# A state-space block followed by a feed-forward block: where three GpSimd steps and three groups of transfers stand in a hand-written order

## The chip, the cores and the metric

The kernel runs on one core of one Trainium2 chip. The metric is the device time of one launch in microseconds; the time before is the median of three runs.

## The reference

Two blocks, one after the other. The first is a chunked state-space scan over 4 sequences with 8 heads each, 768 positions, head width 32, state width 16. The second is a feed-forward layer over the 3072 tokens that come out of it (256 wide, 2048 hidden). Cut to what matters:

```python
for c in range(nc):                      # chunks of positions, state carried along
    L = np.exp(cum[..., :, None] - cum[..., None, :]) * causal
    M = np.einsum('bhin,bhjn->bhij', Cc, Bc) * L
    y_intra = np.einsum('bhij,bhjd->bhid', M, xc)
    y_inter = np.einsum('bhin,bhnd->bhid', Cc, state) * decay_to_i
    y[:, :, sl] = y_intra + y_inter
    state = decay_full * state + sum_over_j(Bc * decay_from_j, xc)
...
x = y.transpose(0, 2, 1, 3).reshape(B * S, H * D)
h = x @ w_in
out = (h * np.cos(h)) @ w_out
```

## The kernel before, in words

**Tiling.** Positions are cut into 6 chunks of 128, and each chunk into two units of 64, so that there are units 0 to 11. A unit holds 64 positions of all 4 sequences, which is 256 tokens. The feed-forward layer is cut into 96 steps `n`, 16 to a chunk: step `n` takes the 256 tokens of one unit and 256 of the 2048 hidden columns. Chunk 1 (units 2 and 3) is the chunk of steps 16 to 31.

**One step of the feed-forward layer.** `first(n)` (L663) multiplies by w_in on TensorE into `hp`. `wind` (L670 on ScalarE, L676 on VectorE) and `gate` (L685, ScalarE) make the cosine, and `gated` (L690, VectorE) multiplies to `gT`. Two steps later, `second(n)` multiplies by w_out. From step 16 on it is `seven` (L771): the product of two-by-two blocks is made with seven instead of eight multiplications. For these, four combinations of the blocks of w_out, `wd[0]` to `wd[3]` (they live in buffers called `words` in the profile), are made once on GpSimd by `differ_w` (L709), each in two halves, `fore` (columns j 0 to 3) and `hind` (j 4 to 7); and three instructions of `differ` on GpSimd (L715, L717, L718) make the combinations `gd` of `gT` for each step. Inside `seven` the products come in the order 1, 2, 6, 7, 5, 4, 3: the first two need no combination, 6 needs the result of L717, 4 needs `wd[3]`, 3 needs the result of L718. `seven(20)` is the first that reads the `hind` halves; it runs in step 22.

**The scan's part around the change.** Of each unit `k`, two VectorE scans (`decays0`, L375) make its decays `lam`, and `weigh0(k)` (L381, GpSimd) makes `sc`, which is B weighed by the decay to the unit's end. `sums(k)` (L477, TensorE) multiplies `sc` with x to the unit's share of the state. `finish0(3)`, in step 22, runs the products with the old state (L516), then `sums(3)`, `sums(4)` and `sums(5)`, then the products inside the unit (L530). `add`, called in step 23, makes the state after unit 3 on GpSimd (L558, L565); half of it has to go to other partitions, which the four transfers at L567 do (the "exchange"). The result is read by `add_state(4)` (L499, VectorE) in step 28 and `open2(2)` (L621, then `sums(6)` and `sums(7)`, TensorE) at the end of step 29.

**What sets the order.** The order of every engine's instructions is written out by hand, in the loop over `n` at the end of the function; nothing is rescheduled. Nearly all transfers are issued by the sync engine (SP), in that same written order, and a transfer that has to wait for something holds up those behind it. `differ_at` says in which step each half of `differ_w` comes (after `gated(n)` and what follows it). `first_decays` puts the decays of units 4 and 5 in steps 17 to 20, and `decays2` calls `weigh0` as soon as a unit's second scan is written. `load(c, i)` loads B and x of chunk `c` in four parts; for chunk 3 they come in steps 22, 24, 25 and 26, for later chunks in the first four steps of a chunk. The names that the change touches are `load`, `add` inside `finish0`, `differ_at`, `decays2`, and two places in the loop.

Of the kernel before, what the change touches and what calls it, by code (L numbers as in the profile page):

```python
# [25 lines left out]
def kernel(  # L26
# [12 lines left out]
    nc = tc.nc  # L39
# [87 lines left out]
    def load(c, i):  # L127
        if c < NC:
            for s in range(2):
                (load_x if i // 2 else load_b)(2 * c + i % 2, s)  # L130

    def group(q, s):
        return slice(32 * (q ^ s), 32 * (q ^ s) + 32)
# [245 lines left out]
    def weigh0(k):  # L379
        scs[k] = sc = scan.tile([P, 2 * H, N], FP32, tag="sc0", bufs=3, name="sc0")  # L380
        G.tensor_tensor(out=sc, in0=bs[k].rearrange("p q (h n) -> p (q h) n", h=H),  # L381
                        in1=lams[k].rearrange("p q h i -> p (q h) i")[:, :, W - 1:W]
                        .to_broadcast([P, 2 * H, N]), op=ALU.mult)
# [119 lines left out]
    def finish0(k):  # L503

        m, xk = m_of[k], xrs[k]
        y = [pair("y") for _ in range(2)] if k else [pair("y")]
        at_ = [[(y[t][:, s, p * W:(p + 1) * W] if k else
                 y[0][:, s, t * P + p * W:t * P + (p + 1) * W]) for p in range(2)]
               for t in range(2) for s in range(2)]
        if k:  # L510
            old = states0.pop(k)
            for p in range(2):
                for s in range(2):
                    for q in range(4):
                        r, c0 = slice(32 * q, 32 * q + 32), W * (q % 2)
                        PE.matmul(at_[2 * (q // 2) + s][p][c0:c0 + W], lhsT=old[r, s, p],  # L516
                                  rhs=rTs[k][r, 2 * p + s], start=(p == 0), stop=False,
                                  tile_position=(32 * q, c0), skip_group_check=True)
        sums(k, [y[0][:, s, 3 * P:] for s in range(2)], lambda q, s: slice(32 * q, 32 * q + 32),
             start=(k == 0))  # L520
        if k == 3:
            at = [y[1][:, s, 2 * P:] for s in range(2)]
            for i in range(2):
                sums(4 + i, [ap[:, i * P:(i + 1) * P] for ap in at], group)
        for p in range(2):
            for t in range(2):
                for s in range(2):
                    ss = slice(s * W, (s + 1) * W)
                    for q in range(4):
                        PE.matmul(at_[2 * t + s][p][32 * q:32 * q + 32],  # L530
                                  lhsT=xk[ss, p, 4 * t + q], rhs=m[ss, p, 4 * t + q],
                                  start=False, stop=True,
                                  tile_position=(s * W, 32 * q), skip_group_check=True)
        if k % 2 == 0:
            yT[k // 2] = two.tile([P, 2, 2, 2 * P], FP32, tag="yT", name="yT")
        t_ = yT[k // 2][:, k % 2]
        if k:
            for t in range(2):
                ACT.copy(out=t_[:, t].rearrange("p (s i) -> p s i", s=2), in_=y[t][:, :, 0:P])
        else:  # L540
            ACT.copy(out=t_.rearrange("p t (s i) -> p s t i", s=2),
                     in_=y[0][:, :, 0:2 * P].rearrange("p s (t i) -> p s t i", t=2))
        if k == 3:
            take_sums(2, at)
        states0[k + 1] = new = states.tile([P, 2, 2, 2 * D], FP32, tag="state0", bufs=2,
                                           name="state0")

        def take():
            for t in range(2):
                ts = slice(t * D, (t + 1) * D)  # L550
                ACT.activation(new[:, :, :, ts], y[0][:, :, 3 * P:].rearrange(
                    "p s (q d) -> p s q d", q=2)[:, :, :, ts], AF.Copy, scale=slot[:, t:t + 1])

        def add():
            dec = scan.tile([P, 2, 2, 2 * D], FP32, tag="whole", bufs=1, name="whole")
            r4 = reachs[k].rearrange("p (q s) i -> p s q i", s=2)
            for s in range(2):
                G.tensor_tensor(out=dec[:, s], in0=old[:, s],  # L558
                                in1=r4[:, s, :, W:].to_broadcast([P, 2, 2 * D]), op=ALU.mult)
            if k < 3:  # L560
                G.tensor_tensor(out=new, in0=new, in1=dec, op=ALU.add)
                return
            whole = states.tile([P, 2, 2, 2 * D], FP32, tag="state1", bufs=1, name="state1")
            for s, to_ in ((1, new), (0, whole)):
                G.tensor_tensor(out=to_[:, s], in0=new[:, s], in1=dec[:, s], op=ALU.add)  # L565
            for q in range(4):
                nc.sync.dma_start(out=whole[group(q, 1), 1], in_=new[group(q, 0), 1])  # L567
            after[3] = whole
        return take, add

    def reaches(c, b):
# [302 lines left out]
    def store_a(dst, src):  # L874
# [4 lines left out]
    piece = {n: ("in", (n + 3) // 2) if n % 2 else ("out", n // 2) for n in range(NF)}  # L879
    fore, hind = slice(0, NJ // 2), slice(NJ // 2, NJ)  # L880
    differ_at = {NF - 2: [(0, fore), (1, fore)], NF - 1: [(2, fore), (3, fore)],
                 **{NF + i + i // 3 * 2: [(i, hind)] for i in range(4)}}

# [3 lines left out]
    def units_at(n, i):  # L889
        return [k for k, at in unit_at.items() if at[i] == n]  # L890
# [45 lines left out]
    def decays2(k, p):  # L936
        decays0(k, p)
        if p == 1:
            if k + 2 < 2 * NC:
                load_arow(k + 2)  # L940
            if k != 2 * NC - 1:
                weigh0(k)

    def reaches2(c, s):
# [61 lines left out]
    for n in range(AHEAD, NC * NF + LAG):  # L1006
        c, f = divmod(n, NF)
        if n < NC * NF:

            if c > 0 and f in (loads_of := (6, 8, 9, 10) if c == 1 else (0, 1, 2, 3)):  # L1010
                load(c + 2, loads_of.index(f))
            if n in (NF - 4, NF - 3):
                load_arow(n - NF + 8)
            if n == NF - 2:
                for k in (4, 5):
                    for s in range(2):
                        load_x(k, s)
            if n in (NF - 1, NF):
                load_along(2, (2 * (n == NF), 2 * (n == NF) + 1))
            for e, i in chunks_at(n, "along"):  # L1020
                load_along(e + 1, (2 * i, 2 * i + 1))
            first(n)
            closing = f == NF - 1 and 1 <= c < NC - 1
            take_y = finish2(c + 1) if closing else None
            wind(n)
            if closing:
                take_y(0)
            for e, s in chunks_at(n - 1, "turn"):
                turn2(e, s)
            for k in units_at(n, 2):  # L1030
                turn_unit(k)
            if n + 1 in piece:
                rests_of.append(grade(*piece[n + 1], later=True))
            gate(n)
            while len(rests_of) > (n == AHEAD):
                rest = rests_of.pop(0)
                if rest:
                    rest()
            joins = n in piece and piece[n] in held
            if joins:  # L1040
                join(*piece[n])

            behind = [lambda at=at: decays2(*at) for at in decays_at(n)]
            behind += [lambda c=c, i=i: add_state(2 * c + i) for c, i in chunks_at(n, "state")
                       if 2 * c + i < 2 * NC - 1]
            behind += [lambda at=at: reaches2(*at) for at in chunks_at(n, "reach")]
            behind += [lambda at=at: turn_blocks(*at) for at in chunks_at(n, "turn")]
            behind += [lambda k=k, p=p: decays0(k, p) for k, at in unit_at.items()
                       for p in range(2) if at[0][p] == n]
            behind = [lambda k=2 * c + i, q=q: weights(k, q) for c, i in chunks_at(n, "weigh")  # L1050
                      for q in range(2)] + behind
            behind = [lambda k=k: weights(k, 1) for k in units_at(n - 1, 3)] + behind
            if not joins and behind:
                behind.pop(0)()
            gated(n)
            if closing:
                take_y(1)
            if add_s and (n == NF - 5 or units_at(n - 1, 4)):
                add_s()
                add_s = None  # L1060
            for do in behind:
                do()
            if f not in ((10, 11, 12) if c == 1 else (10, 11)):
                for do in unsummed:
                    do()
                unsummed.clear()
            for k, ((_, last_), *_) in unit_at.items():
                if last_ == n:
                    weigh0(k)
# [54 lines left out]
```

## Time and profile before

| what | value |
|---|---|
| median of 3 runs | 371.26 us (371.24 to 373.31) |
| profiled execution | 371.67 us, span 369.3 us, clock of TensorE 0.999 |
| PE busy | 359.9 us, 97% of the span |
| PE weight loads | 324.2 us, 88% |
| VectorE (DVE) busy | 249.1 us, 67% |
| GpSimd (POOL) busy | 205.8 us, 56% |
| ScalarE (ACT) busy | 178.0 us, 48% |
| chain that ended last | PE 82%, POOL 5%, DVE 4%, DMA 2%, SPq 2%, ACT 2%, issue 2% |

PE is TensorE's matmuls, PEld its weight loads, SPq the issuing of transfers by the sync engine. The chain that ended last is followed back from the last instruction: at each step to what released it, or to the instruction before it on its engine. A group is a line, an engine and an operation, with the tile written and the tiles read. A wait view says which engine's line sat idle until which other engine's line was done. The window view gives busy time by engine in stretches of the span; the timeline gives single instructions, with start, duration and the idle time before them. All times inside a run count from the start of its span.

### The profile page before, as it was taken

How to read it: one execution, taken by the hardware profiler on the slowest of the kernel's cores; microseconds unless marked ns; L12 is line 12 of the kernel's file. 1: busy time of each engine (PE TensorE's matmuls, PEld its weight loads, DVE VectorE, ACT ScalarE, POOL GpSimd, SP SyncE). 2: the span in 40 equal slices, each digit the busy share in tenths (PEclk: the TensorE clock that was granted, in tenths of full speed). 3: DMA queues.
4: the chain of work that ended last, by engine and by line, in shares of the span. 5: the costliest groups of instructions: out<-in, count | busy, mean ns of one | idle time of the engine just before them, and what ended most of it. 6: DMA issues, size and time to landing. Idle time of an engine off the chain costs nothing.

```text
span 369.3 us, 9744 instructions
## 1 busy us (share of the span) xinstructions
PE 359.9 (97%) x3902; PEld 324.2 (88%) x3902; DVE 249.1 (67%) x420; ACT 178.0 (48%) x324; POOL 205.8 (56%) x327
## 2 busy tenths in 40 slices
PE   7999999999799999999999999999999999999995
PEld 4688888888699889999989999999999999999995
DVE  7689988588857855877754777663776463543463
ACT  4588756463264335444436544435454434444442
POOL 6567656679837734456743445834454453554451
PEclk9999999999999999999999999999999999999999
DMA  8996947682722743614224131010010010010011
GB/s 141 270 351 132 204 110 123 109 128 58 150 43 33 126 85 62 104 50 83 52 46 59 32 73 27 2 38 10 7 26 0 2 30 2 2 28 1 2 28 30
DMA packets 97324, 26.39 MB, mean 71 GB/s; under 512 B 87328, under 2 KB 93184, under 8 KB 97280
## 3 DMA queue, kind: packets, MB, share of 16 engines
q1 hardware_dynamic: 96032, 25.38, 33.9%
q8 instruction: 31, 0.51, 0.6%
q10 hardware_dynamic: 1248, 0.39, 0.5%
q14 instruction: 13, 0.11, 0.1%
HBM read 22.36 MB, written 3.34 MB: 70 GB/s over the span
## 4 chain that ended last, share of the span: by engine, by line
PE 82%; POOL 5%; DVE 4%; issue 2%; DMA 2%; SPq 2%; ACT 2%; POOLq 0%; ACTq 0%; DVEq 0%
PE hp L663 39%; PE o L771 31%; PE o L733 5%; PE y L633 2%; POOL words L709 1%; PE g L607 1%; POOL gd L717 1%; POOL gd L715 1%; DVE mag L261 1%; DMA bc<-in_B_dram 1%; PE y L477 1%; DMA xr<-in_x_dram 1%; DVE mag L263 1%; POOL gd L718 1%; DVE w L676 1%
## 5 line engine op out<-in xcount | busy, mean ns | idle before, releaser
L663 PE MATMUL hp<-yT,w_in 128*128 128x256 f32 x768 | 182.8, 381 | 0.3 <-DVE gT L690 0.3
L663 PEld LDWEIGHTS hp<-yT,w_in 128*128 128x128 f32 x768 | 139.4, 190 | 18.5 <-issue 1.5
L715 POOL TENSOR_TENSOR gd<-gT 128x256 f32<-128x256 f32 x79 | 58.2, 737 | 117.5 <-DVE gT L690 112.1
L676 DVE SCALAR_TENSOR_TENSOR w<-hp,k 128x512 f32<-128x512 f32 x96 | 66.1, 689 | 75.2 <-ACT k L670 75.0
L685 ACT ACTIVATE w<-w,quarter 128x512 f32<-128x512 f32 x96 | 69.4, 723 | 72.5 <-DVE w L676 72.4
L670 ACT ACTIVATE k<-hp 128x512 int32<-128x512 f32 x96 | 57.2, 596 | 95.2 <-PE hp L663 94.8
L690 DVE TENSOR_TENSOR gT<-hp,w 128x512 f32<-128x512 f32 x96 | 65.6, 683 | 35.7 <-ACT w L685 32.9
L771 PE MATMUL o<-words,gd 128*128 128x128 f32 x474 | 66.1, 276 | 0.4 <-POOL gd L717 0.3
L771 PEld LDWEIGHTS o<-words,gd 128*128 128x128 f32 x474 | 59.3, 192 | 0.8 <-POOL gd L717 0.8
L771 PEld LDWEIGHTS o<-w_out,gT 128*128 128x128 f32 x316 | 47.2, 191 | 4.2
L771 PE MATMUL o<-w_out,gT 128*128 128x128 f32 x316 | 48.4, 276 | 0.0
L718 POOL TENSOR_TENSOR gd<-gT,gd 128x128 f32<-128x128 f32 x79 | 44.9, 569 | 6.2
L717 POOL TENSOR_TENSOR gd<-gT,gd 128x128 f32<-128x128 f32 x79 | 39.5, 500 | 6.2
L771 PE MATMUL o<-words,gT 128*128 128x128 f32 x158 | 30.6, 276 | 1.8 <-POOL words L709 1.8
L771 PE MATMUL o<-w_out,gd 128*128 128x128 f32 x158 | 30.5, 275 | 0.0
L733 PE MATMUL o<-w_out,gT 128*128 128x256 f32 x128 | 29.9, 379 | 0.0
L375 DVE TENSOR_TENSOR_SCAN lam<-arow,unit 128x512 f32<-128x512 f32 x20 | 28.7, 1436 | 0.0
L733 PEld LDWEIGHTS o<-w_out,gT 128*128 128x128 f32 x128 | 24.2, 190 | 3.3
L771 PEld LDWEIGHTS o<-words,gT 128*128 128x128 f32 x158 | 24.0, 192 | 2.0 <-POOL words L709 2.0
L771 PEld LDWEIGHTS o<-w_out,gd 128*128 128x128 f32 x158 | 24.0, 192 | 0.0
L788 DVE TENSOR_TENSOR sum<-ps,sum 128x256 f32<-128x256 f32 (+1 forms) x27 | 16.6, 639 | 0.6
L465 DVE TENSOR_TENSOR m<-g,lam 128x512 f32<-128x512 f32 x24 | 16.1, 680 | 0.5 <-PE g L456 0.5
(106 smaller groups left out, 270.6 us busy)
## 6 DMA issues: line engine op xcount, KB each, us to landing
words<-in_moe_w_in_dram SPq DMA_DIRECT2D x8, 512.0 KB
words<-in_moe_w_out_dram SPq DMA_DIRECT2D x8, 512.0 KB
xr<-in_x_dram SPq DMA_DIRECT2D x24, 128.0 KB
arow<-a_cut SPq DMA_DIRECT2D x10, 256.0 KB
arow<-a_cut SPq DMA_DIRECT2D x10, 252.0 KB
out_dram<-sum SPq DMA_DIRECT2D x18, 128.0 KB
bc<-in_B_dram SPq DMA_DIRECT2D x24, 64.0 KB
blocks<-in_B_dram SPq DMA_DIRECT2D x16, 32.0 KB
```

The lines of the kernel that those rows point to most:

```text
L375: V.tensor_tensor_scan(out=lams[k][:, p, hs].rearrange(flat), data0=rows_.rearrange(flat), data1=unit0[:, hs].rearrange(flat), initial=0.0 ...
L663: PE.matmul(to_[:, e], lhsT=w_in[:, k, fs], rhs=y[:, k], start=(k == 0), stop=(k == KT - 1), skip_group_check=True)
L670: ACT.activation(k, hp[n], AF.Copy, bias=0.25, scale=INV_2PI)
L676: V.scalar_tensor_tensor(out=w, in0=hp[n], scalar=INV_2PI, in1=k, op0=ALU.mult, op1=ALU.subtract)
L685: ACT.activation(cos, cos, AF.Sin, bias=quarter, scale=TWO_PI)
L690: V.tensor_tensor(out=gT[n], in0=hp.pop(n), in1=cos, op=ALU.mult)
L715: G.tensor_tensor(out=d[:, 0:2], in0=g[:, 1:2].to_broadcast([P, 2, P]), in1=g[:, 3::-3], op=ALU.subtract)
L717: G.tensor_tensor(out=d[:, 2], in0=g[:, 0], in1=d[:, 0], op=ALU.subtract)
L718: G.tensor_tensor(out=d[:, 3], in0=g[:, 2], in1=d[:, 2], op=ALU.subtract)
L733: PE.matmul(o[c, u][:, t], lhsT=g[:, 2 * e + t], rhs=w_out[:, 2 * j + e], start=(j == e == t == 0), stop=(j == NJ - 1 and e == 1), skip_gr ...
L771: PE.matmul(at[q], lhsT=a_[q], rhs=w[q], start=(j == 0 and q in starts), stop=(j == NJ - 1), skip_group_check=True)
L788: V.tensor_tensor(out=dst, in0=a_, in1=b_.to_broadcast([P, dst.shape[1], P]), op=ALU.add)
```

## The change

Four edits, none of which adds or removes an instruction of an engine or a transfer.

1. `differ_w(3, hind)` moves from step 21 to step 19.
2. `weigh0(4)` moves from step 18 (ahead of `differ(18)`) to step 20 (behind `differ(20)`), `weigh0(5)` from step 20 to step 21 (behind `differ(21)`).
3. The four transfers of the exchange leave `add` in step 23 and are issued in step 25. The GpSimd instructions of `add` stay in step 23.
4. The four parts of a chunk's load, B, B, x, x, become B, x, x, B, and for chunk 3 they come in steps 22, 23, 24, 25 instead of 22, 24, 25, 26.

```diff
     def load(c, i):
         if c < NC:
             for s in range(2):
-                (load_x if i // 2 else load_b)(2 * c + i % 2, s)
+                (load_x if i in (1, 2) else load_b)(2 * c + i // 2, s)
...
-            for q in range(4):
-                nc.sync.dma_start(out=whole[group(q, 1), 1], in_=new[group(q, 0), 1])
             after[3] = whole
+
+            def exchange():
+                for q in range(4):
+                    nc.sync.dma_start(out=whole[group(q, 1), 1], in_=new[group(q, 0), 1])
+            return exchange
         return take, add
...
     differ_at = {NF - 2: [(0, fore), (1, fore)], NF - 1: [(2, fore), (3, fore)],
-                 **{NF + i + i // 3 * 2: [(i, hind)] for i in range(4)}}
+                 **{NF + i: [(i, hind)] for i in range(4)}}
...
         if p == 1:
             if k + 2 < 2 * NC:
                 load_arow(k + 2)
-            if k != 2 * NC - 1:
+            if 5 < k < 2 * NC - 1:
                 weigh0(k)
...
-            if c > 0 and f in (loads_of := (6, 8, 9, 10) if c == 1 else (0, 1, 2, 3)):
+            if c > 0 and f in (loads_of := (6, 7, 8, 9) if c == 1 else (0, 1, 2, 3)):
                 load(c + 2, loads_of.index(f))
...
             gated(n)
             if closing:
                 take_y(1)
+            if n in (NF + 4, NF + 5):
+                weigh0(n - NF)
             if add_s and (n == NF - 5 or units_at(n - 1, 4)):
-                add_s()
+                exchange = add_s()
                 add_s = None
+            if n == NF + 9:
+                exchange()
```

## Prediction

> **What bounds the kernel now.** I read the page first, then the window view by stage, the waits inside the two stages where PE is not full, and the timeline there. The page says that PE is the bound.
>
> ```profile
> span 369.3 us, 9744 instructions
> ...
> PE 359.9 (97%) x3902; PEld 324.2 (88%) x3902; DVE 249.1 (67%) x420; ACT 178.0 (48%) x324; POOL 205.8 (56%) x327
> ```
>
> So a change of order can only win back the few microseconds in which PE waits. The window view, cut at PE's own borders (columns: stretch, its length, busy time by engine), finds them around the change:
>
> ```profile
> 84.00:102.34 18.34, 16.16 (x309) 14.32 (x307) 14.76 (x24) 5.31 (x9) 16.24 (x23) 1.00 0.52 103
> 102.34:126.89 24.55, 24.55 (x223) 22.69 (x218) 18.49 (x28) 12.98 (x27) 15.49 (x25) 1.00 0.38 62
> 126.89:129.69 2.80, 1.97 (x129) 1.52 (x129) 1.91 (x5) 0.72 (x1) 0.88 (x3) 1.00 0.67 105
> ```
>
> PE lacks 2.18 us in the first stretch and 0.83 in the third, and nothing between. In the first, the waits view of 85 to 103 names POOL, and POOL is the busiest engine there (16.24 of 18.34):
>
> ```profile
> PEld o L771 <- POOL words L709: 2.0, 1, 2.0
> PE o L771 <- POOL words L709: 1.8, 1, 1.8
> PEld o L771 <- POOL gd L717: 0.8, 2, 0.5
> ```
>
> The timeline shows what stands in POOL's queue and what slows it (start, duration, engine, line):
>
> ```profile
> 86.65 1.56 POOL L381 TENSOR_TENSOR sc<-bc,lam 128x256 f32<-128x256 f32 x1
> 91.97 1.31 POOL L717 TENSOR_TENSOR gd<-gT,gd 128x128 f32<-128x128 f32 x1
> 95.67 0.64 POOL L381 TENSOR_TENSOR sc<-bc,lam 128x256 f32<-128x256 f32 x1
> 98.02 1.27 POOL L709 TENSOR_TENSOR words<-w_out,words 128x512 f32<-128x512 f32 x1
> 86.10 1.67 DVE L375 TENSOR_TENSOR_SCAN lam<-arow,unit 128x512 f32<-128x512 f32 x1
> 91.82 1.22 DVE L375 TENSOR_TENSOR_SCAN lam<-arow,unit 128x512 f32<-128x512 f32 x1
> 99.35 0.49 PE L771 MATMUL o<-words,gT 128*128 128x128 f32 x2 [1.78 <-POOL words L709]
> 100.61 1.11 PE L477 MATMUL y<-xr,sc 64*32 64x64 f32 x92
> ```
>
> The last combination of w_out ends at 99.29 and PE goes on at 99.35. The sc of units 4 and 5, done early, are read only from 100.9 on. In the third stretch PE waits for x of unit 7, whose transfer is issued late because SP stood 5.4 us before the exchange:
>
> ```profile
> 111.88 3.73 SPq L567 DMA_DIRECT2D state<-state  x4
> 119.61 1.33 SPq L123 DMA_DIRECT2D xr<-in_x_dram  x2
> 125.16 1.32 SPq L123 DMA_DIRECT2D xr<-in_x_dram  x2
> 129.33 0.43 PE L477 MATMUL y<-xr,sc 64*32 64x64 f32 x24 [0.26 <-DMA xr<-in_x_dram]
> ```
>
> **What the Trainium skill says.** "SBUF — State Buffer", section "Who interferes with whom": a VectorE instruction with two SBUF inputs contends with a GpSimd instruction that reads SBUF, and whichever holds the shared ports keeps them for its whole length. The trace agrees: L717 at 91.97, begun 0.15 us into a scan, took 1.31 us instead of 0.46 and ended 0.24 after the scan. "PSUM — Partial Sum Buffer", section "Engine vs sequencer instructions": GpSimd's queue is strictly first in, first out, and matmuls start in program order; the POOL and PE rows agree, so what matters is which item is last in POOL's queue when PE asks. "DMA: Bandwidth & Descriptors", section "Anatomy of one DMA — SWDGE (gpsimd) path": a semaphore wait happens on the issuing sequencer, ahead of dispatch. SP's 5.4 us before L567 agree, with everything behind it held.
>
> **Edits 1 and 2, POOL's order.** I take POOL's costs as start to start. A set of three gd is 1.75 (96.27 to 98.02; the one of step 20 1.83), a half of L709 is 1.24 (89.92 to 91.16; the last 1.27), an sc is 0.60 (95.67 to 96.27), the memset 0.06. Being caught by a scan adds 0.92 (sc at 86.65) and 0.86 (L717 at 91.97). From 86.65 on, before: sc4 1.52, gd(18) 1.75, half 2 1.24, gd(19) 2.61, gd(20) 1.83, memset 0.06, sc5 0.60, gd(21) 1.75, half 3 1.27: it ends at 99.3, without idle time. After, in the changed order: gd(18) takes over the first scan's hit, 2.67, to 89.32; half 2 to 90.56; gd(19) with the second hit 2.61, to 93.17; half 3 to 94.41; gd(20) to 96.24; sc4 to 96.84; memset 96.90; gd(21) to 98.65; sc5 0.63, to 99.28. POOL does the same work, so the last item still ends at 99.3, but now it is sc5, which PE needs later than the words.
>
> Then PE. `hp` of step 20 ends at 88.77 as before. A step's `hp` takes 1.73 and its seven products 1.56; product 6 comes 0.44 after the first, product 3 1.34. gd from L717(18) is done at 88.84, needed at 89.21: the wait of 0.27 goes. seven(18) ends 90.33, `hp` 92.06. L717(19) is done at about 91.83, needed at 92.50: that wait of 0.47 goes; L718(19), caught by the scan, is done at 93.17, needed at 93.40. seven(19) ends 93.62, `hp` 95.35, L717(20) is done at 95.68, needed at 95.79; the words are there since 94.41, so the 1.95 us go too. seven(20) ends 96.91, L516 runs from 97.0 to 97.63. Each of the three sums takes 0.32 (0.96 for the three): sc4 is needed at 97.95, done at 96.84; sc5 is needed at 98.27 but done at 99.28. A new wait of 1.0 us stands here, and behind it in PE's queue the products L530 and the next `hp`. From the start of the last sums to the next `hp` it was 102.34 less 101.25, 1.09; so `hp` of step 23 starts at 99.34 plus 1.09, 100.43 instead of 102.34. Gain 1.91. L530's result is copied by ACT for step 24, 3.3 us later, so nobody else is held up. For POOL not to idle, gT(21) must be there by 96.90; it was done at 96.0, and half 3 now lies over the four reach scans ahead of it, which under the same overlap took 2.02 instead of 1.48 (at 97.78 and at 93.93): 96.4 at worst.
>
> **Edits 3 and 4, SP's order.** The two steps that waited took 2.80 (126.89 to 129.69); the same instructions a chunk later, 185.70 to 187.40, took 1.70. To be won: 1.10. After, x of unit 6 stands in step 23, right behind the blocks (L147) that SP had issued at 106.8; these waited for the VectorE transposes of step 22 (100.31), which I expect about 1.3 us earlier: 105.5. The last reader of its buffer, L530 of unit 3, ends near 100.4, so it does not wait. Five pairs at about 1.3 us each (x of 6, blocks, x of 7, blocks, B of 7) bring SP to the exchange at about 112, when POOL's L565 (112.2 less 1.9) is done. x of unit 7 is issued near 109 and, at the 3.5 us that it took from 125.81, lands by 113; PE asks at 126. The exchange lands at about 118 (3.73 issuing, some 2 more) as before; L499 asks at 125.37 less 1.9: 5 us of slack. B of unit 7 is issued near 111 instead of 117, before its sc at 123. So nothing of the moved transfers gets late. In later chunks x comes a step or two earlier and the second B later; B of unit 9 then stands behind the wait of an output transfer (151.87) and is read some 25 us later: nothing. What is late next at step 29: the state of L499, done at 127.04, is read by the second half of L621 at 127.3, 0.26 us of slack, as both move with PE.
>
> **Sum.** 1.91 plus 1.10 is 3.0 us: span 366.3 instead of 369.3, the profiled execution 368.7 instead of 371.67. The median of the runs lies 0.41 below the profiled execution; with it, 368.3.
>
> **Rivals.** First, POOL escapes a scan: if L718(19) starts just before the scan of 91.82 (it misses by 0.08), VectorE waits instead, POOL is 0.86 earlier, and sc5 comes at 98.4, when PE wants it. Then the stage gives 2.8 to 2.98, the total is 3.9 to 4.1, and the time 367.2. For: starts are that close; against: then w(21) and gT(21) shift. Second, a third hit: an L715 of step 21 under a reach scan, or gT(21) later than 96.9. Sc5 is 0.9 to 1.9 later; the total is 2.1 to 1.1, the time 369.2 to 370.2. For: half 3 presses on the reach scans; against: gd beside these short scans took 0.50 at most. Third, slower: sc5 becomes the chain itself. From 101.25 on (when PE read it before) edits 1 and 2 cost; from 102.35 on they eat edit 4 as well. It needs sc5 3.1 us later than my sum, which means three or four scans' hits or a gT(21) at 100; at 103.5 the time is 372.5. Against: no idle time of POOL in my sum, and slack of 0.5 us at gT(21). Fourth, no effect: L771 at step 22 or L477 at 128.8 waits for something else than named; PE's rows go on 0.06 after the words and 0.04 after the landing of x, which speaks against it; 371.
>
> **How the numbers follow.** Forecast case 0.57 (367.7 to 369.0), first rival 0.18, second 0.18, third 0.04, fourth 0.03. The predicted time is that of the forecast case. The range reaches from the first rival's 367.2 to the second's 370.2, with 0.3 more on each side, since median and profiled run differ by 0.4. One per cent, 3.7 us, is what a measurement of this kernel can tell from no change: below 367.55 lies most of the first rival, 0.16; slower by as much, above 374.97, 0.02.
>
> **What would show it.** Right: no wait of L771 for words or gd between 85 and 100; a wait of about 1 us of PE at L477 for POOL's sc; step 23's `hp` at about 100.4; no wait for x at step 29, x of unit 7 issued before the exchange. Wrong: POOL idle before gd(21), a wait of L771 for gd(19) or gd(20), L477's wait above 2 us or absent, or SP standing before x of unit 6.

## The result, and the profile after

The changed kernel takes 369.14 us (median of 6 runs, 368.51 to 369.53), beside 372.64 us for the kernel before on the same chip: a ratio of 0.991, with a 95% interval of 0.9884 to 0.9937. The prediction, 368.3 against 371.26, was a ratio of 0.992. The profiled execution took 369.53 us with a span of 367.1. Line numbers in the changed kernel are three higher from the end of `add` on: L666 is `hp`, L774 the seven products, L712 `differ_w`, L718, L720 and L721 are `gd`.

The head of the page, after:

```profile
span 367.1 us, 9744 instructions
...
PE 359.2 (98%) x3902; PEld 324.6 (88%) x3902; DVE 251.0 (68%) x420; ACT 177.7 (48%) x324; POOL 205.7 (56%) x327
```

The same busy time stands in a shorter span. The window view (stretch, its length, busy time of PE, PEld, DVE, ACT and POOL, then clock, DMA share and GB/s), cut at PE's borders in this execution (start of step 23's `hp`, of step 24's `hp`, end of step 29's products, start of step 30's `hp`):

```profile
84.00:100.44 16.44, 15.63 (x307) 14.03 (x306) 15.08 (x24) 5.31 (x9) 15.66 (x22) 1.00 0.54 110
100.44:104.79 4.35, 3.55 (x28) 3.26 (x24) 1.63 (x4) 4.17 (x12) 0.52 (x2) 1.00 0.38 57
104.79:125.95 21.16, 21.16 (x198) 19.53 (x196) 17.13 (x25) 8.80 (x15) 15.46 (x24) 1.00 0.60 102
125.95:127.58 1.63, 1.63 (x129) 1.47 (x128) 0.82 (x2) 0.72 (x1) 0.59 (x2) 1.00 0.85 105
```

In the first stretch PE lacks 0.81 us instead of 2.18; in the last, step 29's share of the scan, nothing instead of 0.83. But the second stretch, full before, lacks 0.80 us. The waits view of 84 to 102 no longer names the words, and names sc instead:

```profile
PEld y L477 <- POOL sc L381: 1.0, 1, 1.0
PE y L477 <- POOL sc L381: 0.8, 1, 0.8
```

The timeline of the changed kernel, in the places that were shown of the kernel before (POOL's queue, PE, SP):

```profile
86.53 1.65 POOL L718 TENSOR_TENSOR gd<-gT 128x256 f32<-128x256 f32 x1
...
91.78 1.39 POOL L721 TENSOR_TENSOR gd<-gT,gd 128x128 f32<-128x128 f32 x1
93.13 1.27 POOL L712 TENSOR_TENSOR words<-w_out,words 128x512 f32<-128x512 f32 x1
...
98.65 0.63 POOL L381 TENSOR_TENSOR sc<-bc,lam 128x256 f32<-128x256 f32 x1
...
99.34 0.46 PE L477 MATMUL y<-xr,sc 64*32 64x64 f32 x32 [0.81 <-POOL sc L381]
...
103.79 0.72 PE L774 MATMUL o<-words,gd 128*128 128x128 f32 x5 [0.80 <-issue]
...
105.50 1.64 SPq L123 DMA_DIRECT2D xr<-in_x_dram  x2
...
108.38 1.34 SPq L123 DMA_DIRECT2D xr<-in_x_dram  x2
...
113.45 2.52 SPq L570 DMA_DIRECT2D state<-state  x4
```

The words are done at 94.40, sc of unit 5 at 99.28, and PE goes on at 99.34. Both transfers of x are issued ahead of the exchange. The line at 103.79 is what nothing in the prediction speaks of: PE stops in the middle of `seven(21)`, and no engine or transfer is named ("issue").

### The profile page after: what moved, and what is told of

The parts are those of the page before. It is cut to its first block, busy times and chain, and to the rows that moved or that the text cites. A ratio compares the mean times of both kernels' runs of the same rounds, so it can differ in the third digit from the quotient of the medians.

```text
span 367.1 us, 9744 instructions
## 1 busy us (share of the span) xinstructions
PE 359.2 (98%) x3902; PEld 324.6 (88%) x3902; DVE 251.0 (68%) x420; ACT 177.7 (48%) x324; POOL 205.7 (56%) x327
## 4 chain that ended last, share of the span: by engine, by line
PE 84%; POOL 5%; DVE 4%; issue 2%; ACT 2%; DMA 1%; SPq 0%; POOLq 0%; ACTq 0%; DVEq 0%
PE hp L666 40%; PE o L774 32%; PE o L736 5%; PE y L636 2%; POOL gd L718 1%; POOL words L712 1%; PE g L610 1%; POOL gd L720 1%; DMA bc<-in_B_dram 1%; DVE mag L261 1%; PE y L624 1%; DVE mag L263 1%; PE y L477 1%; DVE w L679 1%; PE g L456 1%
## 5 line engine op out<-in xcount | busy, mean ns | idle before, releaser
L666 PE MATMUL hp<-yT,w_in 128*128 128x256 f32 x768 | 182.8, 382 | 0.3 <-DVE gT L693 0.3
L666 PEld LDWEIGHTS hp<-yT,w_in 128*128 128x128 f32 x768 | 139.8, 191 | 18.1 <-issue 1.2
L718 POOL TENSOR_TENSOR gd<-gT 128x256 f32<-128x256 f32 x79 | 58.8, 744 | 115.8 <-DVE gT L693 109.8
L774 PE MATMUL o<-words,gd 128*128 128x128 f32 x474 | 66.2, 276 | 0.8 <-issue 0.8
L774 PEld LDWEIGHTS o<-words,gd 128*128 128x128 f32 x474 | 59.3, 192 | 1.1 <-issue 0.9
L774 PEld LDWEIGHTS o<-w_out,gT 128*128 128x128 f32 x316 | 47.2, 191 | 4.1
L774 PE MATMUL o<-w_out,gT 128*128 128x128 f32 x316 | 48.5, 276 | 0.0
L721 POOL TENSOR_TENSOR gd<-gT,gd 128x128 f32<-128x128 f32 x79 | 44.9, 569 | 6.2
L720 POOL TENSOR_TENSOR gd<-gT,gd 128x128 f32<-128x128 f32 x79 | 39.3, 498 | 6.2
L774 PE MATMUL o<-w_out,gd 128*128 128x128 f32 x158 | 30.6, 276 | 0.0
L774 PE MATMUL o<-words,gT 128*128 128x128 f32 x158 | 30.6, 276 | 0.0
L774 PEld LDWEIGHTS o<-w_out,gd 128*128 128x128 f32 x158 | 24.0, 192 | 0.0
L774 PEld LDWEIGHTS o<-words,gT 128*128 128x128 f32 x158 | 24.0, 192 | 0.0
```

The lines of the kernel that those rows point to most:

```text
L666: PE.matmul(to_[:, e], lhsT=w_in[:, k, fs], rhs=y[:, k], start=(k == 0), stop=(k == KT - 1), skip_group_check=True)
L718: G.tensor_tensor(out=d[:, 0:2], in0=g[:, 1:2].to_broadcast([P, 2, P]), in1=g[:, 3::-3], op=ALU.subtract)
L720: G.tensor_tensor(out=d[:, 2], in0=g[:, 0], in1=d[:, 0], op=ALU.subtract)
L721: G.tensor_tensor(out=d[:, 3], in0=g[:, 2], in1=d[:, 2], op=ALU.subtract)
L774: PE.matmul(at[q], lhsT=a_[q], rhs=w[q], start=(j == 0 and q in starts), stop=(j == NJ - 1), skip_group_check=True)
```

## The experiments

The start of step 20's `hp` itself lies between 86.5 and 88.5 us in these profiles, before anything that was changed can act on PE, so spans of single executions differ by a microsecond or two for that alone. The stages are therefore compared from that point: A is from step 20's `hp` to step 23's, S from step 23's to step 24's, B from step 24's to step 30's. "Packet" is the start of the one transfer of q8 near this point, to about 0.05 us, counted from step 23's `hp`. The DMA view lists q8 as an instruction queue; this transfer is a single packet of 16 KB. That it brings TensorE's next instructions is not written in any view. It is inferred from what follows. All values but the ratios are of one profiled execution each.

| kernel | A | S | B | packet | ratio to before (95%) |
|---|---|---|---|---|---|
| before | 15.40 | 3.39 | 23.96 | -0.34 | |
| after | 13.62 | 4.35 | 22.79 | +0.46 | 0.991 (0.9884 to 0.9937) |
| e1 edits 1, 2 | 13.61 | 3.39 | 23.76 | -0.32 | 0.9928 (0.9905 to 0.995) |
| e2 edits 3, 4 | 15.39 | 3.39 | 22.90 | -0.53 | 0.9973 (0.9961 to 0.9986) |
| e3 edits 1, 3, 4 | 13.49 | 4.74 | 22.90 | +0.74 | 0.9935 (0.9909 to 0.996) |
| e4 sc5 early | 12.58 | 4.41 | 22.79 | +0.72 | 0.9937 (0.9911 to 0.9963) |
| e5 after again | 13.62 | 3.55 | 22.84 | -0.20 | 0.9927 (0.9903 to 0.9951) |
| e6 rows late | 13.57 | 3.39 | 22.96 | -1.37 | 0.993 (0.9905 to 0.9954) |
| e7 e4 and e6 | 12.57 | 3.39 | 22.83 | -0.22 | 0.991 (0.9887 to 0.9933) |
| e8 edit 4 | 15.38 | 3.39 | 22.91 | -0.31 | 0.9978 (0.9965 to 0.999) |
| e9 edit 2 | 16.03 | 3.39 | 24.17 | -0.92 | 1.0017 (1.0 to 1.0033) |
| e10 edit 3 | 16.00 | 4.15 | 22.98 | -1.09 | 0.9966 (0.9952 to 0.9981) |
| e11 sc5 later | 16.35 | 5.28 | 23.01 | -2.90 | 1.0022 (1.0004 to 1.0041) |
| e12 rows twice | 13.63 | 4.75 | 22.79 | +0.87 | 0.9955 (0.9942 to 0.9969) |

**e1, the order of GpSimd alone.** The diffs of edits 1 and 2 on the kernel before:

```diff
-                 **{NF + i + i // 3 * 2: [(i, hind)] for i in range(4)}}
+                 **{NF + i: [(i, hind)] for i in range(4)}}
...
-            if k != 2 * NC - 1:
+            if 5 < k < 2 * NC - 1:
...
+            if n in (NF + 4, NF + 5):
+                weigh0(n - NF)
```

> Edits 1 and 2 alone (order of GpSimd), the transfers as before. If the two halves of my sum are separate, the profile shows no wait for words, a wait of about 1 us for sc, step 23's hp 1.9 us earlier than before (102.34), and still the wait for x at step 29, which may grow, since x comes when it came and PE asks 1.9 us sooner: up to 1.1 + 1.9 if the transfers of x do not move with PE, so that the time is then that of before; if they move with it, span 367.4 and a gain of 1.9. Rival: edits 1 and 2 give the whole 2.2 us by themselves, span 367.1.

A is 1.79 us shorter, with the wait of PE for sc in it; the wait for x stays, but 0.2 shorter. The span, 367.0, is close to the rival's 367.1, but it is 1.9 us shorter than before from step 20's `hp` to the end, and the rest was won ahead of that point, where no edit acts on PE yet. The timeline of e1:

```profile
99.02 0.46 PE L477 MATMUL y<-xr,sc 64*32 64x64 f32 x32 [0.72 <-POOL sc L381]
...
126.30 0.32 PE L477 MATMUL y<-xr,sc 64*32 64x64 f32 x8 [0.33 <-DMA xr<-in_x_dram]
126.92 0.43 PE L477 MATMUL y<-xr,sc 64*32 64x64 f32 x24 [0.30 <-DMA xr<-in_x_dram]
...
109.67 3.17 SPq L567 DMA_DIRECT2D state<-state  x4
...
122.42 1.32 SPq L123 DMA_DIRECT2D xr<-in_x_dram  x2
```

The exchange starts at 109.67 instead of 111.88: the transfers move with PE, because SP waits for GpSimd's `add`, which moves with PE.

**e2, the order of the transfers alone.** Edits 3 and 4 as in the change, GpSimd's order as before; against the changed kernel:

```diff
-                 **{NF + i: [(i, hind)] for i in range(4)}}
+                 **{NF + i + i // 3 * 2: [(i, hind)] for i in range(4)}}
...
-            if 5 < k < 2 * NC - 1:
+            if k != 2 * NC - 1:
...
-            if n in (NF + 4, NF + 5):
-                weigh0(n - NF)
```

> Edits 3 and 4 alone (order of the transfers), GpSimd as before. If the sum is right: waits for words and gd between 85 and 100 as before (about 3 us with what they cost around them), no wait for x at step 29, span 1.1 us shorter than before, 368.2. Rival: without the earlier PE nothing is won here, since x of unit 7 was late only because of the last few transfers; span 369.3.

A is as before and B 1.06 shorter, with no wait for x. The two halves of the sum are separate.

**e8 and e10, the halves of that half.** The diff of e8 on the kernel before is edit 4, that of e10 edit 3:

```diff
-                (load_x if i // 2 else load_b)(2 * c + i % 2, s)
+                (load_x if i in (1, 2) else load_b)(2 * c + i // 2, s)
...
-            if c > 0 and f in (loads_of := (6, 8, 9, 10) if c == 1 else (0, 1, 2, 3)):
+            if c > 0 and f in (loads_of := (6, 7, 8, 9) if c == 1 else (0, 1, 2, 3)):
```

```diff
-            for q in range(4):
-                nc.sync.dma_start(out=whole[group(q, 1), 1], in_=new[group(q, 0), 1])
...
+            return exchange
...
+            if n == NF + 9:
+                exchange()
```

> Edit 4 alone (order and steps of the loads), the exchange in step 23 and GpSimd as before. If x of unit 7 was late only because it stood behind the exchange and three other pairs, it is now issued one pair behind the exchange, near 117 to 118, lands near 122, and the wait at step 29 is gone: 1.1 us, the same as edits 3 and 4 together; edit 3 is then worth nothing on top. Rival: the exchange's wait of 5.4 us still holds x back past 127; then less than 1.1 is won.

> Edit 3 alone: the exchange in step 25, the loads in their order and steps of before (B, B, x, x in 22, 24, 25, 26), GpSimd as before. x of unit 6 now stands ahead of the exchange and x of unit 7 behind it, the rows and one pair of blocks; the pairs that stood before SP's wait now run during it. x of unit 7 is issued near 120 and lands near 124; the wait at step 29 is gone, 1.1 us, as with edit 4 alone. Rival: x of unit 7 stays behind the exchange as before and is just as late, nothing or half is won.

Each alone takes the wait for x away: B is 1.05 and 0.98 shorter, against 1.06 with both. In both, x of unit 7 is issued behind the exchange; the lines of e8 and of e10:

```profile
116.94 1.36 SPq L123 DMA_DIRECT2D xr<-in_x_dram  x2
```
```profile
120.17 1.32 SPq L123 DMA_DIRECT2D xr<-in_x_dram  x2
```

PE asks at 128 to 130. In the kernel before, six pairs of transfers were issued between the exchange and x of unit 7 (not the three that the expectation of e8 names); e8 leaves one of them there and e10 two. It was enough to take four or five pairs from ahead of x, and either edit makes the other superfluous. (A and S of e10 hold a spell of half clock, on which more below.)

**e3 and e9, edit 2 taken out, and alone.** e3 keeps `weigh0` where it was, with edits 1, 3 and 4; e9 has only `weigh0` moved. The diff of e9 on the kernel before; e3 is the changed kernel with these lines taken back:

```diff
-            if k != 2 * NC - 1:
+            if 5 < k < 2 * NC - 1:
...
+            if n in (NF + 4, NF + 5):
+                weigh0(n - NF)
```

> Edits 1, 3 and 4, the sc of units 4 and 5 where they were before (steps 18 and 20). By my account of GpSimd's queue: the first hit by a scan falls on sc4 again, L717 of steps 18 and 19 are late by 0.27 and 0.47 us again, but sc5 is done near 97.5 and PE does not wait for it; step 23's hp at about 100.4, the same as with edit 2. So edit 2 is worth nothing: span 367.1 as in the changed kernel. Rival: edit 2 is what frees GpSimd for the words; without it 0.7 us or more are lost, span 367.8 to 368.

> Edit 2 alone: sc of units 4 and 5 in steps 20 and 21, the words in step 21, the transfers as before. If GpSimd's queue is what I took it for, gd of steps 18 and 19 come in time again (the waits of 0.27 and 0.47 us go), but the last half of the words is still the last item of the queue, at 99.3; PE stops there longer by what it gained ahead of it, and from step 20's hp to step 23's hp it takes 15.4 us as before: nothing is won. Rival: sc's early place is what made the words late, and 1 us or more is won.

e3's A is 13.49, no longer than with edit 2: the gain in A is edit 1's. PE waits for gd of step 19 instead (0.30) and not for sc. e9 wins nothing; the waits for gd go, and the wait for the words grows by what was won ahead of it, from 1.78 us to 2.81, as the line of e9 shows:

```profile
99.83 0.49 PE L771 MATMUL o<-words,gT 128*128 128x128 f32 x2 [2.81 <-POOL words L709]
```

It even lost 0.6 in A: 0.13 because the words came later, and 0.5 in the small products behind the wait, for which I have no cause.

**e4 and e11, sc of unit 5 earlier and later.** In e4, sc5 follows sc4 in step 20; in e11 it stands behind gd of step 22.

```diff
-            if 5 < k < 2 * NC - 1:
+            if 4 < k < 2 * NC - 1:
...
-            if n in (NF + 4, NF + 5):
-                weigh0(n - NF)
+            if n == NF + 4:
+                weigh0(4)
```

```diff
-            if n in (NF + 4, NF + 5):
-                weigh0(n - NF)
+            if n in (NF + 4, NF + 6):
+                weigh0(4 if n == NF + 4 else 5)
```

> The changed kernel with sc5 directly behind sc4 in step 20 (ahead of gd of step 21), so that PE has no wait of 1 us for sc. In the changed kernel PE stood 0.97 us once more, at 102.8, with nothing named as the cause. Theory one: that stop belongs to PE's instruction packet of the queue q8, which lands at 100.9, just when the row transfer for the decays (L165, issued at 96.4) has drained; then PE gets to the same point 1 us sooner and stands there 1 us longer, about 1.9 us, and the span stays at 367.1. Theory two: that stop is a thing of one execution or moves with PE; then 1.0 us is won, span 366.1.

> The changed kernel with sc5 moved one step further, behind gd of step 22. One more set of gd (1.75 us) then stands ahead of it in GpSimd's queue: sc5 ends near 101.0 instead of 99.3, PE's wait for it grows from 1.0 to about 2.7, and from step 20's hp to step 23's hp it takes 15.3 us, as before the change: edits 1 and 2 are cancelled. Rival: gd of step 22 and sc are hidden, since PE waits for something else at that point; then 13.6 as in the changed kernel.

e4's A is 1.04 shorter than the changed kernel's, with no wait for sc: the new wait was worth what the prediction said. The stop in S did not grow by 1 us, as theory one had it with a packet fixed at 100.9, but stayed at 1.02, while the packet came at 101.75 in an execution that ran 1.6 us late from its start. So e4 does not separate the theories; its ratio shows no gain over the changed kernel's either. e11's wait is 3.11 instead of 2.7, since GpSimd also stood 0.48 us for `gT` of step 22. Its time is 0.2% longer than before, but that is not the wait alone: TensorE ran at half clock behind it (last section). At full clock, with 1.09 us from the last sums to step 23's `hp` and 3.39 for S, I estimate A at 15.9 and A, S and B together at 42.3, which is 0.5 below the 42.75 of the kernel before; the other 2.35 us are the clock's. In e11:

```profile
102.10 0.68 PE L477 MATMUL y<-xr,sc 64*32 64x64 f32 x32 [3.11 <-POOL sc L381]
...
103.65 3.78 PE L666 MATMUL hp<-yT,w_in 128*128 128x256 f32 x8
```

**e5, e6, e7 and e12, the stop in step 23.** e5 is the changed kernel again. The row transfer (L165) loads `arow`, from which the scans make a unit's decays. e6 issues that of unit 7 in step 24 instead of 20; e7 is e4 and e6 together; e12 pulls the row transfer of unit 8 up behind that of unit 7.

```diff
-            if k + 2 < 2 * NC:
+            if k + 2 < 2 * NC and k != 5:
                 load_arow(k + 2)
...
+            if n == NF + 8:
+                load_arow(7)
```

```diff
-            if k + 2 < 2 * NC:
+            if k + 2 < 2 * NC and k != 6:
                 load_arow(k + 2)
+            if k == 5:
+                load_arow(8)
```

> The changed kernel once more, with nothing altered, to see whether PE's stop at step 23 (0.97 us, nothing named) comes again. If the stop comes from the instruction packet of q8 waiting for the drain of the row transfer, it is there again, with the packet 0.4 us or more behind the start of step 23's hp; if it is an accident of one execution, it is gone and the stretch from step 20's hp to the end is 279.3 instead of 280.3 us.

> The changed kernel with the row transfer for unit 7 (L165, 252 KB) issued in step 24 instead of step 20, so that it no longer lies over the stretch 96 to 101. Theory one (the row transfer holds up PE's instruction packet): the packet starts about 0.3 us ahead of step 23's hp, as in the runs without a stop, the stop is gone, and 0.8 to 1.0 us are won: from step 20's hp to the end 279.3. Theory two (the stop is bound to the order of PE's own instructions, or to chance): the packet's place and the stop stay; 280.3.

> Both: sc5 directly behind sc4 in step 20, and the row transfer for unit 7 in step 24. If the wait for sc (1.0) and the stop (0.9) are separate and each is removed by its own edit, from step 20's hp to the end it takes 278.3 us, 2.0 less than the changed kernel, and the time is about 0.5% below the changed kernel's. If PE's instruction packet becomes the next bound because PE is there earlier, the stop comes back with up to 1 us and 279.3 is left.

> The changed kernel with the row transfer for unit 8 (256 KB) pulled from step 25 to directly behind that for unit 7 in step 20, so that the stretch ahead of PE's instruction packet of step 23 carries two of them. If the packet waits for the transfers issued ahead of it to drain (in the runs so far it started at 99.3 without a row transfer there, between 99.8 and 101.8 with one), it now starts 2 to 3 us later, near 103, and PE stands 2 to 3 us in the middle of seven(21) or earlier; the span is 2 us or more longer than the changed kernel's. Rival: the packet's place is chance or PE's own; it starts near 100 to 101 as before, the stop is 0 to 1.3 us and the span stays between 366.4 and 367.2.

The stop of the first profile (0.96) was 0.16 in the second of the same kernel, so most of it belongs to that execution; but it is no accident without a cause. The DMA view of the windows 100.90 to 100.95 of the changed kernel, 99.30 to 99.35 of e6 and 101.40 to 101.45 of e12 holds the one packet:

```profile
q8 instruction: 1, 0.02, 176.0%
```
```profile
q8 instruction: 1, 0.02, 116.5%
```
```profile
q8 instruction: 1, 0.02, 181.8%
```

The percentage is the packet's time as a share of 16 engines over 0.05 us, so it took 1.41, 0.93 and 1.45 us. PE's stop in e12:

```profile
104.28 0.72 PE L774 MATMUL o<-words,gd 128*128 128x128 f32 x5 [1.20 <-issue]
```

What orders the executions is the end of this packet. In the changed kernel it ends at 102.32 and PE goes on at 103.79; in e12 it ends at 102.86 and PE goes on at 104.28. In all five executions with a stop PE goes on 1.41 to 1.56 us after the packet's end, at the same product of `seven(21)` (one product later in e3). In the other nine PE comes to that product 1.56 us or more after the packet's end, and does not stop. Counted by its start, all executions with a packet 0.46 to 0.87 behind step 23's `hp` stop for 0.96 to 1.36 us; e5 (0.20 ahead, 0.16) and e7 (0.22 ahead, none) lie too close together to tell apart in this way. So I take the stop to be PE waiting for this packet: all 14 executions agree with it, though no view names it.

What places the packet is less sure. Counted from step 20's `hp`, it starts at 12.2 us in e6 and 12.4 in e7, which have the row transfer moved away. It starts at 13.3 to 14.3 in the changed kernel, e3, e4 and e5, and at 14.5 in e12, which has two. The order is the expected one, but the two executions of the changed kernel alone differ by 0.6. In e12 the packet did not wait until the DMA engines had drained, as I had expected (they were full until 104), and the stop was 1.36 us instead of 2 to 3. The span is 0.5 and 1.2 us longer than in the two profiles of the changed kernel, not 2. The median of e12's runs, 370.1, is not for the packet alone either, since SP's later transfers are held back too: x of unit 6 is issued at 109.60 instead of 105.50. That the row transfers delay the packet is thus likely, and not more.

e6 alone shows no gain in time (median 369.2, beside 369.1 for e5 on the same chip); its A, S and B together are 0.1 us shorter than e5's. e7 takes the wait for sc and the stop away, and its A, S and B are 1.97 us shorter than the changed kernel's in the first profile, 1.22 than in the second. Its median is the lowest of all, 368.5 against 369.1 for e5, but the intervals overlap. It is the version to take; that it is faster than the changed kernel is seen in these stages of one execution and not shown for the time.

## Why the prediction was right, and which of its steps were not

**The order of GpSimd.** The sum start to start, with each scan's hit moved to the instruction that now lies under it, gave sc5 at 99.28 and step 23's `hp` at 100.43. Measured: 99.28 and 100.44. That it agrees to 0.01 is in part luck: GpSimd began gd of step 21 at 96.80, 0.1 earlier than in the sum, and took 0.1 longer for it. The two hits fell where they were put, on gd of step 18 at 86.53 and on the last gd of step 19 at 91.78, 0.07 behind the start of its scan: the first rival missed by that much. The new wait of 1.0 us for sc is there, and e4 shows its price, 1.04. The gain in A is 1.78 against 1.91, since in this execution step 20's `hp` began 0.12 earlier.

**The order of the transfers.** 1.10 was predicted; B is 1.17 shorter in the changed kernel and 1.06 with edits 3 and 4 alone. (The instructions a chunk later, from which the 1.70 us were read, lie at 185.63 to 187.33 in the trace; the length is right.) x of unit 6 was issued at 105.50 (predicted 105.5), x of unit 7 at 108.38 (near 109), the exchange at 113.45 (about 112), all without consequence, as predicted.

**What failed in the sum.** The total of 3.0 us took PE to be full between the two places. That failed: step 23 lost 0.96 us in the profiled execution, which is why its span fell by 2.2 and not 3.0; in the second execution it lost 0.16, and A, S and B together were 2.74 shorter than before. The prediction asked what would be late next at step 29, and not at step 23. In the kernel before, the same packet was 0.34 ahead: cover that I had not seen, because no wait showed it.

The runs' ratio, 0.991, is 3.4 us of 372.64 with an interval from 2.3 to 4.3. The predicted 3.0 lies in it, but that is in part luck, since the sum left out a loss and a gain. The loss is the stop. The gain is the granted clock: about a third of the later runs of the kernel before had a lower mean clock and took 0.6 to 1.3 us longer, and none of the changed kernel's runs had it (last section). On the chip of e5, the changed kernel's 369.1 stands beside 371.7 for those runs of the kernel before that had the full clock, which is 2.6 us.

**What the sum did not tell.** It booked edits 1 and 2 together and edits 3 and 4 together. e3 and e9 show that the words' step carries all of the gain in A and that moving sc is worth nothing; e8 and e10 show that either of the transfers' edits would have done.

**The rivals.** None took the forecast's place. The measured 369.14 lies between the forecast case's times (up to 369.0) and the second rival's (from 369.2), but the second's mechanism is absent: GpSimd took no third hit and did not stand idle ahead of gd of step 21. The fourth, that PE waits for something else than named, is excluded by e1 and e2. The third was not reached even in e11: with one set of gd more ahead of it, sc5 is done at 102.05, between the third's 101.25 and 102.35. The gain of edits 1 and 2 is gone there, and the half clock took what was left.

## What to carry to other kernels

Where an engine works through its queue without idle time, and each item costs what it cost before, a reordering does not make the last item earlier; it only chooses which item is last, so put there the one that the bound engine needs latest, and check what that engine asks for next. When a stall is taken out, look at everything that was merely in time behind it, the packets of the engine's instruction queue among them, and at large transfers issued shortly ahead. Try each of several edits alone: here one of each pair added nothing to the other.

## What the runs showed of the hardware that was not expected

A wait of PE can cost more than its length. In e10, with the same wait of 1.79 us for the words as in the kernel before, TensorE's granted clock averaged 0.54 over 101.25 to 104.50, and step 23's `hp` took 2.75 us instead of 1.99. The clock fell only after PE had gone on at 99.76: it was still 1.00 from there to 101.25. In e11, with a wait of 3.11 us, it was 0.50 from 100.85 to 107.30. The window view of e10 and of e11 (the third column from the end is the clock):

```profile
101.25:104.50 3.25, 3.25 (x163) 2.90 (x141) 0.59 (x2) 1.31 (x6) 1.34 (x3) 0.54 0.31 46
```
```profile
100.85:107.30 6.45, 5.20 (x105) 4.31 (x106) 0.00 (x0) 2.21 (x8) 1.12 (x3) 0.50 0.38 56
```

The Trainium skill, "TensorE: Matmul & The Clock Gate", section "Part 1: The HAM clock gate (the "warmup" mystery)", has the clock at half after an idle window of about 3.4 us; in these profiled executions it fell after 1.79 us in e10, and did not after 2.81 us in e9 or 1.78 us in the kernel before. The measurement decides: the length of a wait alone does not settle when the clock falls.

The mean clock of every run shows how often this comes. A mean of 0.995 over 370 us is, by my estimate, 3.7 us at half clock, about one spell like that of e10. The runs fall into two groups, 0.995 or less and 0.998 or more:

| kernels | wait for words or sc in the profile, us | runs with 0.995 or less |
|---|---|---|
| before (beside e1 to e12) | 1.78 | 37 of 114 |
| e2, e8, e10 | 1.77 to 1.79 | 25 of 64 |
| e9 | 2.81 | 8 of 12 |
| e11 | 3.11 | 12 of 12 |
| after, e1, e3 to e7, e12 | 0 to 0.84 | 1 of 60 |

e11 differs from the changed kernel in the place of one instruction, which makes the wait, and every run of it had the lower clock. So the long waits bring the lower clock in some runs. The kernels of the last row, in which the longest stop of PE around the change is 1.20 us, hardly ever show it. In which stretch of the unprofiled runs the clock fell is not seen. In the runs of the kernel before, the group with the lower clock is slower by 0.6 to 1.3 us, by the median on each occasion. The change removes this cost together with the wait, and the profile of the kernel before, taken at full clock, does not show it.
